# First MLP on one Trainium2 core: the down projection on 512-token tiles, the leftover 64 tokens of all batches as a ninth set, and second-MLP weight work in both stages

## The chip, the core and the metric

One NeuronCore of a Trainium2 chip runs the whole program in one launch. The metric is the device time of the launch in microseconds (us), the median of the runs shown. TensorE (PE; its weight loads are shown as PEld) multiplies, ScalarE (ACT) and VectorE (DVE) work on the elements, GpSimd (POOL) does next to nothing here, and SyncE (SP) issues most DMAs; some are issued from ScalarE's queue.

## The reference

Three layers in a row, over 8 batches of 576 tokens, 8 heads of 64:

```python
p_packed = sm_attn(p, k, v)                 # 32 packed queries a head against 576 keys
x = sm_attn(q, p_packed, p_packed)          # 576 queries against the 32 packed ones
g = x @ w_gate                              # 4608 tokens, 512 -> 1536
x = silu(g) * (x @ w_val) @ w_out           # first MLP, 1536 -> 512
h = x @ w_in                                # second MLP, 512 -> 2048
return (h * np.cos(h)) @ w_out2             # 2048 -> 512
```

All in fp32. The result has 4608 rows of 512.

## The kernel before

**Products.** TensorE multiplies in fp32r. A value that must keep its precision is held as two parts, hi (rounded by ScalarE, `split`, line 85) and lo (the difference, made by VectorE), and a product is three matmuls (`PASSES`): hi by hi, hi by lo, lo by hi.

**First MLP.** The loop at line 591 goes over the batches b = 0 to 7, and each batch has two stages. The up stage (`a_up`, line 402) makes, for 12 groups f of 128 hidden features, gate and value products (line 433) of the two halves c of the 576 tokens, 288 columns a matmul; ScalarE makes the silu, VectorE the product h, and the split of h makes `g[f]`, a tile [128, 2, 576] with the hi and the lo part. The down stage (`a_down`, line 478) makes the output in 8 groups n: 4 output blocks o of 128 features by 2 halves c. One group is 12 f by 3 passes, 36 matmuls of 288 columns into one PSUM bank (line 493); ScalarE copies the bank out to the tile `x2e` (line 498) and stores it to the DRAM tensor `x2d` from its own queue (line 499).

**What rides in the down stage.** The attention of batch b+1 is cut into steps that the dictionary `steps` hangs ahead of the groups n: 0 `a_s1`, 2 `a_t`, 3 `a_pp`, 4 `a_ppt`, 5 `a_s2`, 6 `a_wp`. `a_s2` (line 223) begins a long chain that alternates between VectorE and ScalarE (transposes, maximum, exponential, sum, division, transpose, split) and ends in the tiles `a2`; `a_wp` makes the weights `wp` of the next up stage, which multiply the attention's output straight away. In the last batch the steps load `x2d` for the second MLP and split it (`load_x2`, `sums_x2`, `split_x2`). At n = 0 SP is given the loads of v and q of batch b+1 (n = 2 for q in batch 0).

**What rides in the up stage.** `extra` (line 450) is called 24 times in each up stage. In batch 0 it decodes first-MLP weights. In batches 1 to 6 it works on the weights of the second MLP, 64 blocks: every second call stores finished pieces to DRAM (`w2_store`), loads the next raw block (`w2_load`), does up to two waiting splits or sums (`w2_work`) and decodes the present block (`w2_decode`: two ScalarE and two VectorE operations); the other calls do up to one split or sum. `prefetch` loads p and k of the next batch.

**Order.** The whole body stands in `tc.manual_schedule()`: each engine and each DMA queue works in the order of the program text, and an instruction whose input, buffer or queue entry is not ready holds up everything behind it on its engine. Buffers come from pools with a fixed number of slots: 18 of tag "c" (`ct`: g, a2, wp, v and others), 12 of tag "m" (`mt`: k, q, transposed tiles, raw blocks and finished pieces of the second-MLP weights), 11 small ones (`ht`), 8 PSUM banks.

**Second MLP** (from line 735 on): for 6 chunks of 768 tokens, up products of 384 columns (line 685) and down products of 512 columns (line 700).

Of the kernel before, what the change touches and what calls it, by code (L numbers as in the profile page):

```python
# [21 lines left out]
NF1, NF2, KD = DF1 // 128, DF2 // 128, DM // 128  # L22
NPAIR = H // 2
HS = S // 2
NC = -(-S // 128)
SPAD = 128 * NC
TH = 384
# [13 lines left out]
def attention_mlp_kernel(ctx: ExitStack, tc: tile.TileContext, qT, kT, vP, pP, wgv, w1o, w2, out):  # L41
# [11 lines left out]
    dr = ctx.enter_context(tc.tile_pool(name="dr", bufs=1, space=bass.MemoryType.DRAM))  # L53

    x2d = dr.tile([KD, 128, NT], F32, name="x2d")
    w2u = dr.tile([NPF, 7, 128, 512], F32, name="w2u")
    w2d = dr.tile([NF2, 128, 2, 512], F32, name="w2d")

# [6 lines left out]
    def ct(shape, dt, name):  # L65
        return sb.tile(shape, dt, tag="c", name=name, bufs=CBUFS)

    def mt(shape, dt, name):
        return sb.tile(shape, dt, tag="m", name=name, bufs=12)

    def ht(shape, dt, name):
        return sb.tile(shape, dt, tag="s", name=name, bufs=SBUFS)

    def bank(shape, name):
        return ps.tile(shape, F32, tag="b", name=name)
# [237 lines left out]
    def w2_load(i):  # L313
        if i < 4 * NF2:
            w2_raw[i] = raw_words(mt, w2[i // 2, :, 256 * (i % 2):256 * (i % 2) + 256], 256)
# [15 lines left out]
    def w2_decode(i):  # L331
        w_ = ht([128, 256], F32, "w2f")
        t_ = ht([128, 256], F32, "w2t")
        decode_a(w2_raw[i], t_, w_)
        decode_b(w2_raw.pop(i), t_, w_)
        u, half = divmod(i, 2)
        if u >= NF2:
            w2_put(w_, w2d[u - NF2, :, :, 256 * half:256 * half + 256])
            return
        p, a = divmod(u, 2)  # L340
        to = [w2u[p, n].rearrange("p (x c) -> p x c", x=2) for n in range(7)]
        w2_f[a, half] = w_
        if (a, half) == (0, 0):
            w2_put(w_, to[0])
        elif (a, half) == (0, 1):
            w2_put(w_, to[4])
        elif (a, half) == (1, 0):
            w2_sum("s3", (0, 0), ALU.subtract, (1, 0), to[2])
        else:
            w2_sum("s1", (1, 0), ALU.add, (1, 1), to[3])  # L350
            w2_put(w_, to[5])
            w2_sum("s2", "s1", ALU.subtract, (0, 0), to[1])
            w2_sum("s4", (0, 1), ALU.subtract, "s2", to[6])

    def w2_work(n):
        for _ in range(n):
            if w2_todo:
                w2_todo.pop(0)()

    def w2_store():  # L360
        while w2_done:
            p, dst = w2_done.pop(0)
            SP.dma_start(out=dst, in_=p.bitcast(F32))
# [34 lines left out]
    def flush_split():  # L398
        while pend_split:
            pend_split.pop(0)()  # L400

    def a_up(b):
        g = []
        for f in range(NF1):
            gt = ct([128, 2, S], F32R, "g")
            g.append(gt)
            if b > 0:
                if f in (2, 6):
                    a_wp(b, (f // 2 + 1, f // 2 + 2))
                w = [wp[b, f // 2, u][:, :, f % 2] for u in range(2)]  # L410
            else:
                w = wp.pop((0, f))
            banks = [(bank([128, HS], "pg"), bank([128, HS], "pv")) for _ in range(2)]
            if b == 0:
                for u in range(2):
                    for c in range(2):
                        for o, p_ in zip((0, 128), banks[c]):
                            PE.matmul(  # L418
                                out=p_, lhsT=w[:, u, o:o + 128], rhs=a2[u][:, HS * c:HS * c + HS],
                                start=(u == 0), stop=(u == 1),  # L420
                            )
                    if u == (f == 0) and f + 1 < NF1:
                        a_wp0(f + 1)
            for c in range(2):
                sl = slice(HS * c, HS * c + HS)
                pg, pv = banks[c]
                for o, p_ in ((0, pg), (128, pv)):
                    n = 0
                    for u in range(2):
                        if b == 0:  # L430
                            continue
                        for (x, y) in PASSES:
                            PE.matmul(  # L433
                                out=p_, lhsT=w[u][:, x, o:o + 128], rhs=a2[u][:, y, sl],
                                start=(n == 0), stop=(n == 5),
                            )
                            n += 1
                if b == 0 and f > 0:
                    u_step(2, 1)
                s_ = ht([128, HS], F32, "silu")  # L440
                ACT.activation(out=s_, in_=pg, func=AF.Silu)  # L441
                flush_split()
                h_ = ht([128, HS], F32, "h")
                DVE.tensor_tensor(out=h_, in0=s_, in1=pv, op=ALU.mult)  # L444
                pend_split.append(lambda h_=h_, gt=gt, sl=sl: split(h_, gt[:, 0, sl], gt[:, 1, sl]))
                extra(b, f, c)
            prefetch(b, f)
        return g

    def extra(b, f, c):  # L450
        if b == 0:
            u_step(0, 1)
            u_step(1, 1)
            if f == 0:
                u_step(2, 1)
        elif b < B - 1:
            s_ = 24 * (b - 1) + 2 * f + c
            if s_ % 2 == 0 and s_ // 2 < 4 * NF2:
                w2_store()
                w2_load(s_ // 2 + 1)  # L460
                w2_work(2)
                w2_decode(s_ // 2)
            else:
                w2_work(1)

    def prefetch(b, f):
        n = b + 1
        if n >= B:
            return
        if f == 4:  # L470
            load_p(n)
            for j in range(NPAIR):
                load_k(n, j)
        if f == 9 and b == 0:
            for j in range(NPAIR):
                load_v(n, j)

    def a_down(b, g, steps):
        for n in range(8):
            for s_ in steps.get(n, ()):  # L480
                s_()
            if 0 < b < B - 1 and n == 0:
                for j in range(NPAIR):
                    load_v(b + 1, j)
            if b + 1 < B and n == (2 if b == 0 else 0):
                for j in range(NPAIR):
                    load_q(b + 1, j)
            o, c = n // 2, n % 2
            sl = slice(HS * c, HS * c + HS)
            acc = bank([128, HS], "o1")  # L490
            for f in range(NF1):
                for i, (x, y) in enumerate(PASSES):
                    PE.matmul(  # L493
                        out=acc, lhsT=wo[o, f // 4][:, x, f % 4, :], rhs=g[f][:, y, sl],
                        start=(f == 0 and i == 0), stop=(f == NF1 - 1 and i == 2),
                    )
            ev = ht([128, HS], F32, "x2e")
            ACT.activation(out=ev, in_=acc, func=AF.Copy)  # L498
            ACT.dma_start(out=x2d[o, :, S * b + HS * c:S * b + HS * c + HS], in_=ev)

    late = {}

# [49 lines left out]
    with tc.manual_schedule():  # L552
# [37 lines left out]

        for b in range(B):
            g = a_up(b)
            flush_split()
            flush_wo()
            w2_store()
            if b == 0:
                w2_load(0)
            n = b + 1
            steps = {}
            if n < B:  # L600
                steps = {
                    0: (lambda: a_s1(n),),
                    2: (lambda: a_t(n),),
                    3: (lambda: a_pp(n),),
                    4: (lambda: a_ppt(n),),
                    5: (lambda: a_s2(n),),
                    6: (lambda: a_wp(n, (0, 1)),),
                }
            else:
                gates.close()  # L610
                late["x"] = ctx.enter_context(tc.tile_pool(name="xs", bufs=1, side="right", reuse_waits="tile"))
                x_now = [new_xs() for _ in range(7)]
                steps = {0: (lambda: load_x2(0),)}
                for i in range(4):
                    steps[i + 1] = (lambda i=i: sums_x2(i),)

                for i, ns in enumerate(((0,), (3,), (2,), (1, 4), (5, 6))):
                    steps[i + 1] = steps.get(i + 1, ()) + tuple(lambda n=n: split_x2(n, x_now) for n in ns)
            if b == 0:
                for i, k in enumerate((1, 1, 2, 2, 1)):  # L620
                    steps[i] = steps.get(i, ()) + (lambda: u_step(0, 1), lambda: u_step(1, 1), lambda: u_step(2, 1)) * k
                steps[5] = (flush_wo,) + steps[5]
            a_down(b, g, steps)
# [215 lines left out]
```

## Time and profile before

| | us |
|---|---|
| median of 3 runs | 1488.43 (1488.20 to 1488.91) |
| the profiled execution, its own time | 1488.04 |
| its span, first to last instruction of the program | 1486.3 |
| part of the span before the second MLP begins | 738.4 |

The profile is of one execution; its time is that of the launch, 1.7 us more than the span. A row of busy time counts an engine as busy while an instruction of it runs; matmuls overlap their neighbours, so the duration of one is longer than the time from its start to the next one's. The chain of work that ended last is followed back from the last instruction and tells, piece by piece, what the end of the program waited for. In timelines the number in brackets is the idle time of the engine ahead of the row, and who ended it. Batches are counted from 0.

### The profile page before, as it was taken

The page shows a single profiled execution, that of the slowest core. Times are in us where ns is not written, and L with a number is a line of the kernel's source. Part 1 is how long each engine was busy: PE and PEld are TensorE (multiplying, and loading weights), DVE is VectorE, ACT ScalarE, POOL GpSimd, SP SyncE. Part 2 cuts the span into 40 slices and gives each one's busy share as a digit, 9 for nine tenths or more (in the row PEclk, how much of TensorE's full clock was granted, in tenths as well). Part 3 has the DMA queues.
Part 4 walks back from the last instruction along what each step waited for, and adds up shares of the span by engine and source line. Part 5 has one row for each costly group of instructions (what it writes and reads, how often), then busy time and mean ns, then how long its engine had stood idle before and what let it go on. Part 6 is the DMA issues. An engine that isn't in the chain of part 4 may idle for free.

```text
span 1486.3 us, 27615 instructions
## 1 busy us (share of the span) xinstructions
PE 1478.3 (99%) x10476; PEld 1338.7 (90%) x10476; DVE 985.8 (66%) x2048; ACT 839.4 (56%) x1917; POOL 3.0 (0%) x22
## 2 busy tenths in 40 slices
PE   9999999999999999999999999999999999999999
PEld 6689998999899998989989999999999999999997
DVE  6988749485673837355286866776686686677654
ACT  6986737375572736434284645656555564565642
POOL 0000000000000000000000000000000000000000
PEclk9999999999999999999999999999999999999999
DMA  8742616355162542201295586576667558556641
GB/s 328 260 156 86 239 46 226 117 173 195 52 194 75 161 136 89 80 22 43 92 393 178 181 288 197 178 241 204 215 191 256 180 180 290 195 179 195 206 161 43
DMA packets 129411, 257.14 MB, mean 173 GB/s; under 512 B 13568, under 2 KB 37120, under 8 KB 129280
## 3 DMA queue, kind: packets, MB, share of 16 engines
q1 hardware_dynamic: 120064, 245.94, 50.4%
q10 hardware_dynamic: 9216, 9.44, 1.8%
q8 instruction: 83, 1.36, 0.4%
q14 instruction: 48, 0.39, 0.1%
HBM read 213.39 MB, written 41.94 MB: 172 GB/s over the span
## 4 chain that ended last, share of the span: by engine, by line
PE 95%; DVE 2%; ACT 2%; DMA 1%; issue 0%; SPq 0%; ACTq 0%; DVEq 0%
PE acc L700 26%; PE p L685 23%; PE o L493 20%; PE pg L433 9%; PE pv L433 9%; PE wp L386 3%; PE pg L418 1%; PE pv L418 1%; PE pp L203 1%; PE s L229 1%; PE s L151 1%; PE wp L371 0%; DMA qt<-in_qT 0%; PE tp L192 0%; DMA vt<-in_vP 0%
## 5 line engine op out<-in xcount | busy, mean ns | idle before, releaser
L700 PE MATMUL acc<-wd,g 128*128 128x512 f32 x1728 | 413.8, 389 | 0.0
L685 PE MATMUL p<-xs,up 128*128 128x384 f32 x2016 | 372.9, 337 | 1.3 <-ACT p L760 1.3
L700 PEld LDWEIGHTS acc<-wd,g 128*128 128x128 f32 x1728 | 322.4, 188 | 57.1
L685 PEld LDWEIGHTS p<-xs,up 128*128 128x128 f32 x2016 | 353.7, 188 | 12.7 <-ACT p L760 1.6
L493 PEld LDWEIGHTS o<-g,wo 128*128 128x128 f32 x2304 | 306.7, 188 | 13.8 <-DVE d L250 5.0
L493 PE MATMUL o<-g,wo 128*128 128x288 f32 x2304 | 316.6, 296 | 0.3 <-DVE wo L87 0.2
L663 ACT ACTIVATE t<-c,quarter 128x384 f32<-128x384 f32 x144 | 88.4, 614 | 196.7 <-DVE c L773 191.0
L433 PE MATMUL pg<-a,wp 128*128 128x288 f32 x1008 | 162.4, 296 | 0.0
L433 PE MATMUL pv<-a,wp 128*128 128x288 f32 x1008 | 160.6, 294 | 0.0
L433 PEld LDWEIGHTS pg<-a,wp 128*128 128x128 f32 x1008 | 142.4, 188 | 11.7 <-ACT wp L86 8.4
L433 PEld LDWEIGHTS pv<-a,wp 128*128 128x128 f32 x1008 | 143.0, 188 | 0.0
L87 DVE TENSOR_TENSOR g<-h,g 128x288 fp32r<-128x288 f32 x192 | 87.5, 456 | 39.4 <-ACT g L86 39.2
L673 DVE TENSOR_TENSOR g<-t,g 128x384 fp32r<-128x384 f32 x192 | 106.0, 552 | 8.0 <-ACT g L660 7.8
L665 DVE TENSOR_TENSOR t<-t,k 128x384 f32<-128x384 f32 x192 | 106.1, 552 | 3.5 <-ACT k L669 1.8
L768 DVE TENSOR_TENSOR u<-v,p 128x384 f32<-128x384 f32 x48 | 26.6, 554 | 118.2 <-PE p L685 117.9
L441 ACT ACTIVATE silu<-pg 128x288 f32<-128x288 f32 x192 | 78.3, 408 | 42.0 <-PE pg L433 37.5
L666 ACT ACTIVATE t<-t 128x384 f32<-128x384 f32 x192 | 98.2, 512 | 2.6 <-DVE t L665 2.5
L498 ACT ACTIVATE x2e<-o 128x288 f32<-128x288 f32 x64 | 26.5, 413 | 128.3 <-PE o L493 127.9
L660 ACT ACTIVATE g<-t 128x384 fp32r<-128x384 f32 x192 | 98.5, 513 | 0.4 <-DVE t L671 0.4
L86 ACT ACTIVATE g<-h 128x288 fp32r<-128x288 f32 x192 | 85.0, 443 | 24.2 <-DVE h L444 23.8
L669 ACT ACTIVATE k<-t 128x384 int32<-128x384 f32 x192 | 98.2, 511 | 0.0
L444 DVE TENSOR_TENSOR h<-silu,pv 128x288 f32<-128x288 f32 x192 | 86.0, 448 | 16.1 <-PE pv L433 5.9
(95 smaller groups left out, 1346.9 us busy)
## 6 DMA issues: line engine op xcount, KB each, us to landing
up<-w2u SPq DMA_DIRECT2D x336, 256.0 KB, 3.2
wd<-w2d SPq DMA_DIRECT2D x96, 512.0 KB, 6.2
raw<-in_w SPq DMA_DIRECT2D x64, 256.0 KB, 3.2
w2u<-w2p SPq DMA_DIRECT2D x56, 256.0 KB, 2.2
raw<-in_wgv SPq DMA_DIRECT2D x24, 512.0 KB, 7.5
vt<-in_vP SPq DMA_DIRECT2D x32, 320.0 KB, 4.3
kt<-in_kT SPq DMA_DIRECT2D x32, 288.0 KB, 5.0
qt<-in_qT SPq DMA_DIRECT2D x32, 288.0 KB, 6.0
```

Of the source, the lines that this page charges most:

```text
L87: eng.tensor_tensor(out=lo, in0=src, in1=hi.bitcast(F32), op=ALU.subtract)
L433: PE.matmul(out=p_, lhsT=w[u][:, x, o:o + 128], rhs=a2[u][:, y, sl], start=(n == 0), stop=(n == 5),)
L444: DVE.tensor_tensor(out=h_, in0=s_, in1=pv, op=ALU.mult)
L493: PE.matmul(out=acc, lhsT=wo[o, f // 4][:, x, f % 4, :], rhs=g[f][:, y, sl], start=(f == 0 and i == 0), stop=(f == NF1 - 1 and i == 2),)
L660: ACT.activation(out=three["g"][:, 0, :], in_=three["t"], func=AF.Copy)
L663: ACT.activation(out=now["t"], in_=now["h"], func=AF.Identity, scale=1.0 / TWO_PI, bias=quarter)
L665: DVE.tensor_tensor(out=one_["t"], in0=one_["t"], in1=one_["k"], op=ALU.subtract)
L666: ACT.activation(out=one_["t"], in_=one_["t"], func=AF.Sin, scale=SIN_SCALE)
L669: ACT.activation(out=now["k"], in_=now["t"], func=AF.Copy)
L673: DVE.tensor_tensor(out=three["g"][:, 1, :], in0=three["t"], in1=three["g"][:, 0, :].bitcast(F32), op=ALU.subtract)
L685: PE.matmul(out=out, lhsT=w[:, u, 128 * k:128 * k + 128], rhs=x[:, v, k, :], start=(first and k == 0 and i == 0), stop=(last and k == 1 an ...
L700: PE.matmul(out=acc, lhsT=gs[p, a, t][:, x, o:o + 128], rhs=wd[j, f][:, y, :], start=(f == 0 and n == 0), stop=(f == 3 and n == 2),)
```

## The change

The down stage of a batch takes only the first 512 of its 576 tokens, as one tile: 4 groups a batch, one for each output block o, each of 36 matmuls of 512 columns. The bank is copied out in two halves of 256. The other 64 tokens of each `g[f]`, hi and lo, are stored by SP to a DRAM tensor `rest`, 24 DMAs of 32 KB a batch in pieces of 256 bytes. For batches 0 to 6 they are issued in the down stage, after the loads of v and q, at the middle of the first group (for batch 7 during its up stage, each f one turn late). From the up stage of batch 7 on SP also loads the set back as tiles of 8 x 64 = 512 tokens (`load_rest`, 24 DMAs of 256 KB; those of the last three f behind the end of that stage), and `a_rest` runs the down projection on this ninth set ahead of the down stage of batch 7. The attention steps keep their numbers: step n now comes at f = 0 or f = 6 of the group o = n // 2. The second-MLP weight work keeps its 24 calls a batch, 16 of them in the up stage (two of three turns), 8 in the down stage (f = 3 and f = 9 of each group).

```diff
@@ -22,6 +22,8 @@
 NF1, NF2, KD = DF1 // 128, DF2 // 128, DM // 128
 NPAIR = H // 2
 HS = S // 2
+WIN = 512
+REST = S - WIN
 NC = -(-S // 128)
 SPAD = 128 * NC
 TH = 384
@@ -53,6 +55,7 @@
     dr = ctx.enter_context(tc.tile_pool(name="dr", bufs=1, space=bass.MemoryType.DRAM))
 
     x2d = dr.tile([KD, 128, NT], F32, name="x2d")
+    rest = dr.tile([NF1, 2, 128, B, REST], F32, name="rest")
     w2u = dr.tile([NPF, 7, 128, 512], F32, name="w2u")
     w2d = dr.tile([NF2, 128, 2, 512], F32, name="w2d")
 
@@ -398,6 +401,8 @@
     def flush_split():
         while pend_split:
             pend_split.pop(0)()
+
+    gr = []
 
     def a_up(b):
         g = []
@@ -445,7 +450,24 @@
                 pend_split.append(lambda h_=h_, gt=gt, sl=sl: split(h_, gt[:, 0, sl], gt[:, 1, sl]))
                 extra(b, f, c)
             prefetch(b, f)
+            if b == B - 1 and f > 0:
+                store_rest(b, f - 1, g[f - 1])
+                if f > 2:
+                    gr.append(load_rest(f - 3))
         return g
+
+    w2_n = [0]
+
+    def w2_step():
+        s_ = w2_n[0]
+        w2_n[0] += 1
+        if s_ % 2 == 0 and s_ // 2 < 4 * NF2:
+            w2_store()
+            w2_load(s_ // 2 + 1)
+            w2_work(2)
+            w2_decode(s_ // 2)
+        else:
+            w2_work(1)
 
     def extra(b, f, c):
         if b == 0:
@@ -453,15 +475,8 @@
             u_step(1, 1)
             if f == 0:
                 u_step(2, 1)
-        elif b < B - 1:
-            s_ = 24 * (b - 1) + 2 * f + c
-            if s_ % 2 == 0 and s_ // 2 < 4 * NF2:
-                w2_store()
-                w2_load(s_ // 2 + 1)
-                w2_work(2)
-                w2_decode(s_ // 2)
-            else:
-                w2_work(1)
+        elif b < B - 1 and (2 * f + c) % 3 < 2:
+            w2_step()
 
     def prefetch(b, f):
         n = b + 1
@@ -475,28 +490,68 @@
             for j in range(NPAIR):
                 load_v(n, j)
 
+    def store_rest(b, f, gt):
+        for i in range(2):
+            SP.dma_start(out=rest[f, i, :, b, :], in_=gt[:, i, WIN:S].bitcast(F32))
+
+    def load_rest(f):
+        if f < NF1 // 2:
+            r = [mt([128, B, REST], F32R, "gr") for _ in range(2)]
+        else:
+            both = ct([128, 2, B, REST], F32R, "gr")
+            r = [both[:, i] for i in range(2)]
+        for i in range(2):
+            SP.dma_start(out=r[i].bitcast(F32), in_=rest[f, i])
+        return r
+
+    def down_group(o, moving, steps, to, between=None):
+        acc = bank([128, WIN], "o1")
+        for f in range(NF1):
+            if f % (NF1 // 2) == 0:
+                for s_ in steps.get(2 * o + f // (NF1 // 2), ()):
+                    s_()
+            if between and f % 6 == 3:
+                between()
+            for i, (x, y) in enumerate(PASSES):
+                PE.matmul(
+                    out=acc, lhsT=wo[o, f // 4][:, x, f % 4, :], rhs=moving(f, y),
+                    start=(f == 0 and i == 0), stop=(f == NF1 - 1 and i == 2),
+                )
+        for h in range(2):
+            ev = ht([128, WIN // 2], F32, "x2e")
+            ACT.activation(out=ev, in_=acc[:, WIN // 2 * h:WIN // 2 * h + WIN // 2], func=AF.Copy)
+            to(o, h, ev)
+
     def a_down(b, g, steps):
-        for n in range(8):
-            for s_ in steps.get(n, ()):
-                s_()
+        def to(o, h, ev):
+            c0 = S * b + WIN // 2 * h
+            ACT.dma_start(out=x2d[o, :, c0:c0 + WIN // 2], in_=ev)
+
+        def loads(n):
             if 0 < b < B - 1 and n == 0:
                 for j in range(NPAIR):
                     load_v(b + 1, j)
             if b + 1 < B and n == (2 if b == 0 else 0):
                 for j in range(NPAIR):
                     load_q(b + 1, j)
-            o, c = n // 2, n % 2
-            sl = slice(HS * c, HS * c + HS)
-            acc = bank([128, HS], "o1")
-            for f in range(NF1):
-                for i, (x, y) in enumerate(PASSES):
-                    PE.matmul(
-                        out=acc, lhsT=wo[o, f // 4][:, x, f % 4, :], rhs=g[f][:, y, sl],
-                        start=(f == 0 and i == 0), stop=(f == NF1 - 1 and i == 2),
-                    )
-            ev = ht([128, HS], F32, "x2e")
-            ACT.activation(out=ev, in_=acc, func=AF.Copy)
-            ACT.dma_start(out=x2d[o, :, S * b + HS * c:S * b + HS * c + HS], in_=ev)
+            if b < B - 1 and n == 1:
+                for f in range(NF1):
+                    store_rest(b, f, g[f])
+
+        steps = {n: tuple(steps.get(n, ())) + (lambda n=n: loads(n),) for n in range(8)}
+        for o in range(KD):
+            down_group(o, lambda f, y: g[f][:, y, 0:WIN], steps, to, w2_step if 0 < b < B - 1 else None)
+
+    def a_rest(gr):
+        def to(o, h, ev):
+            half = B // 2
+            ACT.dma_start(
+                out=x2d[o].rearrange("p (b n) -> p b n", b=B)[:, half * h:half * h + half, WIN:S],
+                in_=ev.rearrange("p (b n) -> p b n", b=half),
+            )
+
+        for o in range(KD):
+            down_group(o, lambda f, y: gr[f][y].rearrange("p b n -> p (b n)"), {}, to)
 
     late = {}
 
@@ -595,6 +650,12 @@
             w2_store()
             if b == 0:
                 w2_load(0)
+            if b == B - 1:
+                for f in range(len(gr), NF1):
+                    if f == NF1 - 1:
+                        store_rest(b, f, g[f])
+                    gr.append(load_rest(f))
+                a_rest(gr)
             n = b + 1
             steps = {}
             if n < B:
```

## Rows read from the trace of the kernel before

**Rows 1.** The page: span, share of TensorE, and the chain that ended last.

```profile
span 1486.3 us, 27615 instructions
...
PE 1478.3 (99%) x10476; PEld 1338.7 (90%) x10476; DVE 985.8 (66%) x2048; ACT 839.4 (56%) x1917; POOL 3.0 (0%) x22
...
PE 95%; DVE 2%; ACT 2%; DMA 1%; issue 0%; SPq 0%; ACTq 0%; DVEq 0%
```

**Rows 2.** Chain, down of batch 6 to up of 7: start us, us, what.

```profile
613.59 9.74 PE o L493 x72
...
640.37 1.13 PE s L229 x32
641.50 4.99 PE o L493 x36
646.49 1.88 PE wp L386 x32
648.37 9.74 PE o L493 x72
658.10 0.79 PE pg L433 x6
```

**Rows 3.** The same chain, whole span: last down stage, and one 512-wide group.

```profile
700.40 38.16 PE o L493 x288
...
764.61 2.72 PE acc L700 x12
```

**Rows 4.** Busy time by stage, the up stages of batches 2, 3 and 5.

```profile
216.87:260.83 43.96, 43.96 (x385) 39.54 (x384) 40.34 (x105) 34.78 (x98) 0.31 (x2) 1.00 0.64 212
...
305.42:349.44 44.02, 44.02 (x385) 39.54 (x384) 40.41 (x105) 34.96 (x97) 0.31 (x2) 1.00 0.61 205
...
482.22:525.58 43.36, 43.36 (x385) 39.45 (x383) 35.16 (x86) 34.18 (x89) 0.31 (x2) 1.00 0.50 155
```

**Rows 5.** Timeline of ScalarE and VectorE, end of the down stage of batch 6.

```profile
652.82 0.69 ACT L86 ACTIVATE a<-af 128x576 fp32r<-128x576 f32 x1 [3.66 <-DVE af L252]
653.41 0.39 ACT L498 ACTIVATE x2e<-o 128x288 f32<-128x288 f32 x1
...
654.20 2.07 ACT L86 ACTIVATE wp<-wp 128x512 fp32r<-128x512 f32 x4 [0.40 <-ACT x2e L498]
654.83 2.48 DVE L87 TENSOR_TENSOR wp<-wp 128x512 fp32r<-128x512 f32 x4 [0.54 <-ACT wp L86]
```

**Rows 6.** Groups by line: the hi half of a second-MLP weight split.

```profile
L86 ACT ACTIVATE w2p<-w2f 128x256 fp32r<-128x256 f32 x56 | 23.3, 415 | 7.7 <-DVE w2f L108 7.5
```

**Rows 7.** Timeline of the SP queue, the loads at the start of that stage.

```profile
612.13 1.75 SPq L132 DMA_DIRECT2D vt<-in_vP  x4
613.93 2.02 SPq L128 DMA_DIRECT2D qt<-in_qT  x4
```

**Rows 8.** DMA issues: line engine op xcount, KB each, us to landing.

```profile
raw<-in_w SPq DMA_DIRECT2D x64, 256.0 KB, 3.2
w2u<-w2p SPq DMA_DIRECT2D x56, 256.0 KB, 2.2
...
qt<-in_qT SPq DMA_DIRECT2D x32, 288.0 KB, 6.0
...
xb<-x2d SPq DMA_DIRECT2D x24, 384.0 KB, 5.5
```

**Rows 9.** Timeline, last down stage: last g split, x2 splits, weight loads.

```profile
701.82 0.46 DVE L87 TENSOR_TENSOR g<-h,g 128x288 fp32r<-128x288 f32 x1 [0.51 <-ACT g L86]
...
726.83 0.95 DVE L87 TENSOR_TENSOR xs<-xb,xs 128x768 fp32r<-128x768 f32 x1
729.05 19.12 SPq L544 DMA_DIRECT2D up<-w2u  x21
```

**Rows 10.** SP's own waits: weight loads held by landings of ScalarE's stores.

```profile
SPq L544 <- DMA x2d<-x2e: 14.2, 4, 5.7
```

**Rows 11.** The page's DMA queues: packets, MB, share of 16 engines.

```profile
q10 hardware_dynamic: 9216, 9.44, 1.8%
```

## The prediction, written before the changed kernel was run

> **What bounds the kernel now.** I read the page first: TensorE is busy 99% of the span and holds 95% of the chain that ended last [rows 1]. So what counts is how long TensorE works, and whether a change makes it wait. Next the chain in order of time, through one down stage of the first MLP and into the next up stage [rows 2]: every piece but the start of the small steps is a run of matmuls, with no gap between a group of the down projection and the attention step that rides in it. VectorE and ScalarE are hidden there, as long as each step's result is ready when TensorE comes to it. The last down stage, which has no attention steps, gives the clean price of a matmul of 288 columns: 288 of them in 38.16 us, 132.5 ns each; the second MLP gives that of 512 columns: 12 in 2.72 us, 226.7 ns [rows 3].
>
> **1. Fewer, wider matmuls: -11.5 us.** Before: 8 batches x 8 groups x 36 = 2304 matmuls of 288 columns. After: 8 x 4 x 36 for the batches and 4 x 36 for the ninth set, 1296 of 512. The columns are the same, 663,552; what falls away is the part of a matmul's price that doesn't grow with its columns, 1008 times. A batch goes from 38.16 us to 144 x 0.2267 = 32.64 us. 8 x 38.16 = 305.3 becomes 9 x 32.64 = 293.8 [rows 3]: 11.5 us less, all on the path. The granted clock is 1.00, the level of 2.4 GHz, in the up stages shown [rows 4], and I take both prices at that level.
>
> **2. Second-MLP weight work moved: -1.3 us.** The up stages of batches 2 and 3 take 43.96 and 44.02 us, that of batch 5 43.36 us with the lighter half of that work [rows 4]; VectorE is busy 40 of 44 us there and holds TensorE a little. With 16 calls instead of 24 these 0.60 + 0.66 us should go (0 to 1.3). The calls that leave cost TensorE nothing by themselves; what they delay in the down stage is in 3 and 4.
>
> **3. The down stage gets shorter, its chain of steps doesn't: +2.7 us.** From `a_s2` (640.37) to the first up matmul (658.10) TensorE now takes 17.7 us, of it one group of 4.99 and two of 9.74 together [rows 2]. With half groups of 18 x 0.2267 = 4.08 us this is 1.13 + 4.08 + 0.25 (what 4.99 has over 4.74) + 1.88 + 8.16 + 0.26, 15.8 us: TensorE comes 2.0 us earlier to the up stage. What it needs there ends with the split of `wp`: VectorE's four parts start at 654.83 and take 2.48 us, so the second of them, needed by the sixth or so matmul (658.77), is there at 656.07, 2.7 us ahead [rows 5]. ScalarE's side also gets longer: two copies of `x2e` instead of one lie ahead of the `wp` splits, 0.79 us each with their store (653.41 to 654.20) [rows 5], and in batches 1 to 5 one weight split, 0.41 us [rows 6]. 2.7 - 2.0 - 0.79 - 0.41 = -0.5: a wait of 0.5 us in five batches, and of 0.1 us in batches 0 and 6: 2.7 us together. Ends: 0, and 1.5 us each in all seven (if ScalarE's further calls push the next stage's silu as well), 10.5 us.
>
> **4. The 24 stores on SP's queue: +2.5 us.** They come behind eight loads, three stores of finished pieces and a raw load, and ahead of the next raw load, which the decode at f = 3 of o = 2 waits for; behind that decode stand, on ScalarE and VectorE, the transposes of `a_s2`. When is it wanted? `a_s2` now comes 26.78 us behind the first down matmul, 23.7 of it five groups [rows 2]; five halves of 4.08 make it 23.5 us, and f = 3 lies 2.04 before: 21.4 us. When does it land? The eight loads start 1.4 us ahead of the first down matmul and take SP 3.8 us, 0.44 to 0.50 each [rows 2, 7]. At 0.50: 2.4 us, four more DMAs to 4.4, 24 stores to 16.4, three stores and the load to 18.4, landing 3.2 us later [rows 8], 21.6 us. That is within 0.2 us of when it is wanted, so the cover is thin. I take 0.5 us in each of batches 1 to 5, 2.5 us; ends: 0 (0.44 each: 19.7 us) and the first rival's 18.5 us. The stores themselves need only `g`, long done. In batch 0 the last two raw blocks of `w_out` stand behind them; they have the two spare steps up to `a_s2`, and I count 0 (to 2 us).
>
> **5. The ninth set waits for its last piece: +3.0 us.** The last `g` split ends at 702.28, 2.0 us into the stage that follows [rows 9]. Its two stores: 0.9 us to issue, 2.2 to land (nearest row: a store of 256 KB); its two loads: 0.9 and 3.2 [rows 8]: 9.2 us behind the up stage's end. `a_rest` comes to its last f after 33 x 0.2267 = 7.5 us: 1.8 us of wait, once. Four of the last tiles find no free slot until the up stage has ended (12 g, 2 a2 and 4 wp or loaded tiles fill the 18), so six loads of 256 KB stand ahead in the same queue. With 6.0 us, the slowest landing of [rows 8], for both, it would be 8.4 us. I take 3.0, nearer the first, since those six are issued some 3 us before.
>
> **6. Counted at nothing.** The x2 load for the second MLP moves behind the ninth set: 0.8 us to copy out, 2.2 to store, 5.5 to load [rows 8], 8.5 us of a 32.6 us stage; its splits ended 10.6 us before the stage did (727.78 of 738.4) [rows 9] and have no other work beside them. Without that cover it would be the 8.5 us. The first second-MLP weights are loaded from 729.05, when the o = 2 groups end, 9.3 us ahead of use [rows 9]; now 8.2 us, against a landing of 3.2 [rows 8]; without cover, the 1.1 us. 8 copies more on ScalarE lie beside TensorE.
>
> **Sum.** -11.5 - 1.3 + 2.7 + 2.5 + 3.0 = -4.6 us against the profiled execution's 1488.04 (span 1486.3 and 1.7 around it): 1483.4. The median shown, 1488.43, is 0.4 above that execution, so 1483.8. 0.2%, about what a measurement of this kernel tells from no change, is 3.0 us.
>
> **The rivals.** *SP holds the decode (slower, 0.22).* The place is the raw load of 4. If the stores can't start before the eight loads have landed (the last is issued at 615.95 and takes 6.0 us [rows 7, 8], 8.4 us into the stage), 24 x 0.50, four more DMAs and 3.2 us bring the load to 25.6 us, 4.2 late, 3.7 beyond what 4 counts: 5 x 3.7 = 18.5 us, 1502. It decides from about 1 us of lateness in each batch on: five times that eats the gain. For it: SP's queue does wait for earlier landings [rows 10]. Against it: a store has a ninth of a load's bytes.
>
> *ScalarE's own stores queue behind them (slower, 0.05).* A store of `x2e` at the end of o = 0 that has to wait for landings, as SP's loads do for ScalarE's stores, up to 5.7 us [rows 10], would hold `a_t`'s copies: 5 us x 7, some 1519.
>
> *The pieces of 256 bytes are slow (slower, 0.04).* ScalarE's queue moved 9216 packets of about 1 KB in 1.8% of 16 engines' span, 46 ns each [rows 11]; at that price a store's 8 pieces an engine take 0.37 us, less than SP's 0.50. No row shows a piece of 256 bytes. At twice that, 92 ns, the 24 take 17.7 us in place of 12, the raw load lands 5.7 us later, 5.9 late, and five batches cost 27 us more than 4 counts: 1511. The Trainium skill, "DMA: Bandwidth & Descriptors", section "Specifications", speaks for this: below 512 bytes a transfer is read, modified and written. By the packet row alone the stores stay hidden.
>
> *Waits cancel the gain (0.13).* 3, 4 and 5 together some 4 to 7 us more: 1486 to 1491.
>
> *The whole gain (0.1).* 3 to 5 cost nothing: 1475.6. That the columns don't get cheaper is as good as excluded by [rows 3].
>
> **Numbers.** Forecast 0.46, its own range 1479 to 1487. Range for 8 in 10: 1477 to 1500; what is left out is half of the whole gain, the upper half of the first rival, and the two dear ones. Faster by over 0.2%: 0.40 + 0.1 = 0.50. Within: 0.06 of the forecast, 0.10 of the cancelled, 0.04 of the first rival, 0.20. Slower: 0.30.
>
> **What would show it.** 1: 1296 matmuls, 0.227 us apart. 2: up stages of batches 2 and 3 at 43.4 us. 3: a gap of half a us ahead of the first up matmul, ended by a `wp` split. 4: no wait of ScalarE for a raw block over 1 us in the down stages. 5: one gap of 2 to 4 us in the ninth set. Gaps of several us in each down stage would prove the forecast wrong, and so would a second MLP that starts later by more than this sum.

## The result and the profile after

The changed kernel takes 1497.85 us (median of 4 runs, 1496.2 to 1501.04), the kernel of before beside it 1488.32: ratio 1.0066, 95% interval 1.0049 to 1.0084. It was forecast 0.3% faster and is 0.7% slower. The profiled run takes 1497.66 us against 1488.04, so +9.6 where the sum said -4.6.

The page of the changed kernel, the lines that answer to [rows 1]:

```profile
span 1495.8 us, 25963 instructions
...
PE 1477.0 (99%) x9468; PEld 1276.2 (85%) x9468; DVE 988.0 (66%) x2048; ACT 840.9 (56%) x1925; POOL 3.0 (0%) x22
...
PE 81%; DVE 6%; DMA 4%; SPq 4%; ACT 4%; issue 1%; ACTq 0%; DVEq 0%
```

TensorE is still "99% busy"; that line doesn't show the loss. The chain does: TensorE held 95% of it, now 81%, and VectorE, DMAs, SP's queue and ScalarE have taken its place. The second MLP starts at 747.6 us (738.4 before) and takes 0.4 us longer than it did, so nearly all of the loss lies ahead of it. Busy time by stage (columns as in [rows 4]: window, its length, TensorE's busy time, then its weight loads, VectorE, ScalarE, GpSimd, each with its count; granted clock, DMA share, GB/s); a down stage runs from its first matmul of the down projection to the first of the next up stage, so a wait ahead of an up stage counts in the down stage before it. These are the down stages of batches 0 and 2 to 5, the ninth set, and the down stage of batch 7:

```profile
83.73:127.62 43.89, 40.73 (x309) 30.16 (x301) 33.14 (x65) 27.29 (x57) 0.00 (x0) 1.00 0.40 123
255.06:294.51 39.45, 39.31 (x309) 30.10 (x301) 22.10 (x54) 17.44 (x43) 0.00 (x0) 1.00 0.53 173
339.09:379.64 40.55, 39.31 (x308) 30.09 (x300) 22.59 (x55) 17.89 (x45) 0.00 (x0) 1.00 0.51 163
423.95:465.15 41.20, 39.31 (x308) 30.09 (x300) 18.44 (x43) 16.03 (x39) 0.00 (x0) 1.00 0.43 134
510.79:551.23 40.44, 39.31 (x309) 30.09 (x301) 18.57 (x43) 16.03 (x39) 0.00 (x0) 1.00 0.44 136
677.74:714.97 37.23, 34.98 (x147) 27.82 (x145) 1.28 (x3) 2.95 (x8) 0.00 (x0) 0.95 0.33 97
714.97:747.61 32.64, 32.64 (x146) 27.04 (x145) 10.10 (x11) 8.66 (x15) 0.00 (x0) 1.00 0.35 110
```

The last line is the forecast's price, 32.64 us for 144 matmuls. The down stages of batches 1 and 6 take 39.14, which is what a stage with its attention steps costs undisturbed; before it was 44.4. Everything above that is waiting. The chain of waits through the down stage of batch 5 into the next up stage, in order of time (start us, us, what):

```profile
515.08 5.39 DMA rest<-g
...
530.91 0.52 SPq L366
...
531.48 3.24 DMA raw<-in_w
534.74 0.46 ACT w2t L101
...
536.45 1.57 DVE d L239 x4
...
550.58 0.61 ACT wp L89
551.21 0.70 DVE wp L90
551.95 1.00 PE pg L438 x4
```

In place of the unbroken matmuls of [rows 2] the chain runs through a store of `rest`, the rest of that block on SP's queue (left out here), a raw block, the decode (L101), `a_s2`'s VectorE steps (L239 on), the split of `wp`, and only then into the up stage. SP's timeline of that stage (start us, us, what):

```profile
514.32 0.41 SPq L94 DMA_DIRECT2D raw<-in_w  x1
515.08 15.74 SPq L495 DMA_DIRECT2D rest<-g  x24
...
531.48 0.60 SPq L94 DMA_DIRECT2D raw<-in_w  x1
```

The block of 24 stores holds the queue for 15.7 us, and the raw block behind it is issued 20.7 us after the stage's first matmul. ScalarE's waits that a DMA ended (us in total, times, longest):

```profile
ACT w2t L101 <- DMA raw<-in_w: 8.5, 5, 3.2
ACT ET L197 <- DMA rest<-g: 2.8, 3, 1.9
ACT dec L101 <- DMA raw<-in_w1o: 2.5, 1, 2.5
```

The first line is those raw blocks, five times, in batches 1 to 5; the last is batch 0's last raw blocks of `w_out`, behind the stores in the same queue.

### The profile page after: what moved, and what is told of

It is laid out like the page before. It is cut to its first block, busy times and chain, and to the rows that moved or that the text cites. A ratio compares the mean times of both kernels' runs of the same rounds, so it can differ in the third digit from the quotient of the medians.

```text
span 1495.8 us, 25963 instructions
## 1 busy us (share of the span) xinstructions
PE 1477.0 (99%) x9468; PEld 1276.2 (85%) x9468; DVE 988.0 (66%) x2048; ACT 840.9 (56%) x1925; POOL 3.0 (0%) x22
## 4 chain that ended last, share of the span: by engine, by line
PE 81%; DVE 6%; DMA 4%; SPq 4%; ACT 4%; issue 1%; ACTq 0%; DVEq 0%
PE acc L761 26%; PE p L746 22%; PE pg L438 9%; PE pv L438 9%; PE o L516 8%; SPq L495 2%; PE wp L389 2%; DMA rest<-g 2%; PE pg L423 1%; PE pv L423 1%; DMA raw<-in_w 1%; DVE af L255 1%; DVE d L253 1%; DVE d L239 1%; DVE d L243 1%
## 5 line engine op out<-in xcount | busy, mean ns | idle before, releaser
L516 PE MATMUL o<-g,wo 128*128 128x512 f32 x1152 | 273.6, 394 | 0.0
L516 PEld LDWEIGHTS o<-g,wo 128*128 128x128 f32 x1152 | 213.1, 188 | 56.1 <-issue 4.6
L438 PE MATMUL pg<-a,wp 128*128 128x288 f32 x1008 | 167.2, 300 | 6.1 <-ACT wp L89 4.7
L775 DVE TENSOR_TENSOR oacc<-oacc,acc 128x512 f32<-128x512 f32 x108 | 73.7, 683 | 32.2 <-PE acc L761 32.1
```

The costliest lines, as they stand in the source:

```text
L438: PE.matmul(out=p_, lhsT=w[u][:, x, o:o + 128], rhs=a2[u][:, y, sl], start=(n == 0), stop=(n == 5),)
L516: PE.matmul(out=acc, lhsT=wo[o, f // 4][:, x, f % 4, :], rhs=moving(f, y), start=(f == 0 and i == 0), stop=(f == NF1 - 1 and i == 2),)
```

## The experiments

Three theories. **Q**: the block of stores holds SP's queue, and a raw block behind it comes too late. **S**: the shorter stage is too short for its own chain of steps, whatever the queue does. **Ninth set**: its wait for the last piece, with the clock. All times are medians; "before" is the kernel of before, run beside them (medians of 1487.78 to 1488.12).

| run | us | ratio to before, 95% interval |
|---|---|---|
| before, weight work spread (before_spread) | 1486.33 | 0.9990 [0.9981, 0.9999] |
| after, weight work in the up stage (w2_in_up) | 1492.99 | 1.0038 [1.0026, 1.0051] |
| after, stores one by one (stores_spread) | 1489.98 | 1.0013 [1.0004, 1.0021] |
| after, 12 stores (stores_paired) | 1489.45 | 1.0009 [1.0000, 1.0017] |
| after, ninth set later (ninth_after_one) | 1491.32 | 1.0025 [1.0016, 1.0034] |
| after, ninth set kept busy (ninth_busy) | 1494.57 | 1.0045 [1.0033, 1.0058] |
| stores one by one + ninth set later (both_moves) | 1484.55 | 0.9977 [0.9968, 0.9986] |
| + `a_s2` earlier (three_moves) | 1483.18 | 0.9967 [0.9955, 0.9979] |
| + weight work in two groups (four_moves) | 1482.11 | 0.9961 [0.9948, 0.9975] |
| + 12 late stores (five_moves) | 1483.25 | 0.9965 [0.9952, 0.9979] |
| after, weight work in two groups (w2_first_block) | 1528.95 | 1.0277 [1.0263, 1.0291] |

**One part alone, on the kernel of before.** `extra` keeps 16 calls of 24, and each of the eight 288-column groups gets one:

```diff
-        elif b < B - 1:
+        elif b < B - 1 and (2 * f + c) % 3 < 2:
...
             for f in range(NF1):
+                if 0 < b < B - 1 and f == 6:
+                    w2_step()
```

> The kernel of before with one part of the change alone: the second-MLP weight work at 16 calls in the up stage and 8 in the down stage, one in the middle of each of the eight 288-column groups. Prediction's point 2: 1.3 us less, 1487. Theory Q: the same or a little less, since SP's queue is free in that kernel's down stage: 1486.5 to 1488.5. Theory S (decodes, splits and raw waits in the down stage delay the chain of steps by themselves): 1 to 2 us a batch over six batches, 1494 to 1500.

1486.33, 1.5 us faster. Its up stage of batch 3, by busy time; that of batch 2 takes as long:

```profile
304.49:348.01 43.52, 43.52 (x386) 39.61 (x384) 37.29 (x95) 32.40 (x86) 0.31 (x2) 1.00 0.51 176
```

43.52 in both. [rows 4] begin 0.16 us later in the stage; cut as here, the two stages took 44.12 and 44.18 us, so they give 1.26 us. In the down stage of this kernel, still 44.4 us long, decodes and raw loads do no harm by themselves.

**The opposite: the changed kernel without that part.**

```diff
-        elif b < B - 1 and (2 * f + c) % 3 < 2:
+        elif b < B - 1:
             w2_step()
...
-            down_group(o, lambda f, y: g[f][:, y, 0:WIN], steps, to, w2_step if 0 < b < B - 1 else None)
+            down_group(o, lambda f, y: g[f][:, y, 0:WIN], steps, to)
```

> The changed kernel with all 24 calls of the second-MLP weight work back in the up stage, none in the down stage; the 512 columns, the stores and the ninth set stay. Theory Q (the block of 24 stores holds SP's queue, so that the raw block behind it reaches ScalarE late): no decode stands in the down stages 1 to 6 any more, so the 1.5 to 2.3 us that stages 3, 4 and 5 lose go, 5 to 6 us in all, and the up stages cost at most 1 us more: 1492 to 1494. Theory S (the stage of 40.8 us is too short for its own chain of steps, whatever the queue does): with less work in the stage the chain ends earlier as well, but the half-us to one-us waits at the start of the up stages stay: 1494 to 1497. Theory M (moving the work is worth 1.3 us as predicted and the loss is elsewhere): 1499.

1492.99, as theory Q had it. The block of stores is still there, but no decode waits behind it, and the down stages 1 to 6 take 39.12 to 39.20 us; that of batch 4, 41.20 in the changed kernel, by busy time:

```profile
424.62:463.76 39.14, 39.14 (x309) 30.26 (x301) 17.69 (x41) 14.48 (x35) 0.00 (x0) 1.00 0.43 132
```

Against the expectation, the up stages of batches 2 and 3 took 45.4 and 45.8 us: with 24 calls there, VectorE finishes that work after the matmuls and holds the scores (`s`) of the next step. (The profiled execution took 1495.12 us, 2.1 above the median; its ninth set took 39.2 us, with the granted clock at 0.50 over 4 us and 0.70 over the next 3.5.) So a change that gains 1.5 us on the kernel of before costs some 5 us beside the block: they collide.

**The stores one by one**, one every second weight tile (the last argument picks the hi or the lo half):

```diff
-            if b < B - 1 and n == 1:
-                for f in range(NF1):
-                    store_rest(b, f, g[f])
...
+            if each and f % 2:
+                each(6 * o + f // 2)
...
+        each = (lambda k: store_rest(b, k // 2, g[k // 2], (k % 2,))) if b < B - 1 else None
```

> The changed kernel with the 24 stores of batches 0 to 6 issued one by one, one every second weight tile of the down stage, in place of a block at its second eighth. Theory Q: the raw blocks (of w_out in batch 0, of the second MLP's weights in the others) no longer stand behind 24 stores, and no ScalarE wait for raw over 1 us is left in the down stages; batch 0 gives back 3 to 4 us and batches 2 to 5 together 5 to 6: 1488 to 1490. Theory S: the steps are late without the block too, under 3 us come back: 1495 to 1498.

1489.98. The decodes' waits for a second-MLP raw block are gone (a copy of `ET` still waits for one in two batches, 1.1 us at most): the group of decodes on ScalarE (busy, mean ns of one | idle before) reads

```profile
L101 ACT ACTIVATE w2t<-raw 128x256 f32<-128x256 f32 x64 | 27.6, 432 | 0.0
```

and the down stages of batches 2 to 5 take 39.15 to 39.46, batch 0 42.13 in place of 43.89: 1.8 us back, where 3 to 4 were expected. The ninth set got longer here, 39.18 us; the granted clock was at 0.50 over 4 us of it and at 0.73 over the next 4.

**The block with half as many stores**, the same bytes in the same 256-byte pieces:

```diff
-        for i in range(2):
-            SP.dma_start(out=rest[f, i, :, b, :], in_=gt[:, i, WIN:S].bitcast(F32))
+        SP.dma_start(
+            out=rest[f, :, :, b, :].rearrange("i p n -> p i n"), in_=gt[:, :, WIN:S].bitcast(F32)
+        )
```

> The changed kernel with one store for both halves of a g tile: 12 stores of 64 KB in a batch's block in place of 24 of 32 KB, the block still at the second eighth; bytes and pieces stay the same. Theory Q as a matter of issues (each store holds SP's queue for 0.43 to 0.47 us): the block lasts 5 to 6 us less, the raw block lands before the step chain needs it, and nearly all that the spread stores gave back comes here too: 1489 to 1492. Theory Q as a matter of bytes (the queue is held because the pieces of 256 bytes have to land): a store holds twice as long, nothing comes back: 1496 to 1498.

1489.45: what the spread stores gave comes here too. SP's timeline in the down stage of batch 5:

```profile
506.72 0.67 SPq L94 DMA_DIRECT2D raw<-in_w  x1
507.43 10.09 SPq L494 DMA_DIRECT2D rest<-g  x12
...
518.19 0.60 SPq L94 DMA_DIRECT2D raw<-in_w  x1
```

The block lasts 10.1 us, not 15.7, and the raw block is issued 14.8 us into the stage (503.42), not 20.7. Bytes and pieces are the same, so they are not what the block costs: 12 DMAs fewer at some 0.47 us make the 5.7 us. The waits at the head of the block, for landings of the loads ahead, are still there.

**The ninth set.** In the changed kernel's chain, its wait for the last piece:

```profile
680.82 4.58 DMA rest<-g
...
685.46 2.62 DMA gr<-rest
...
688.12 32.00 PE o L516 x133
```

and by busy time the clock around that wait:

```profile
684.00:688.00 4.00, 1.87 (x7) 0.79 (x5) 0.00 (x0) 0.00 (x0) 0.00 (x0) 0.97 0.45 153
688.00:691.50 3.50, 3.38 (x8) 2.53 (x9) 0.00 (x0) 0.77 (x2) 0.00 (x0) 0.54 0.07 23
```

Two edits. One puts the set behind the first group of the last down stage, with x2's loads and splits two eighths later; the other fills the wait with nine matmuls of zeros (`g0` is true for the ninth set alone):

```diff
         for o in range(KD):
+            if b == B - 1 and o == 1:
+                a_rest(gr)
...
-                a_rest(gr)
...
-                steps = {0: (lambda: load_x2(0),)}
+                steps = {2: (lambda: load_x2(0),)}
```

> The changed kernel with the ninth set between the first and the second 512-column group of the last batch's down stage, in place of ahead of it; the loads of x2 and the splits behind them come two eighths later. The last piece then has 8 us more to arrive. If the ninth set's 4.6 us over 144 matmuls are its wait for the last piece and the half-level clock that follows the wait, they all go and the time is 1493 to 1494. If only the wait goes and the clock falls anyway, 1495 to 1496. If the later splits make the second MLP's first matmuls late, that takes back up to 3 us.

```diff
+            if o == 0 and not between and g0 and f == NF1 - 1:
+                keep_busy(9)
```

> The changed kernel with nine matmuls of zeros into a spare bank in the ninth set, ahead of the matmuls on the last piece, where TensorE waits 2.3 us. They add no wait if they end before the piece lands. If the fall of TensorE's granted clock to its half level (0.54 over 3.5 us) comes from that wait, it stays away, and the ninth set takes 1.6 us less than 37.2: 1496. If the clock falls there for another reason: 1497.5 to 1498.5.

The ninth set in the first (1491.32 us) and in the second (1494.57 us), busy time by stage:

```profile
684.47:717.11 32.64, 32.64 (x146) 27.04 (x144) 0.00 (x0) 3.08 (x8) 0.00 (x0) 1.00 0.25 68
```

```profile
674.71:710.77 36.06, 35.65 (x165) 29.04 (x163) 1.28 (x3) 2.95 (x8) 0.00 (x0) 1.00 0.34 99
```

Moved, it costs its matmuls and nothing else: 4.6 us less, and x2's later splits delay nobody. Filled, the clock stays at 1.00 and the set takes 1.2 us less, short of the 1.6 expected. In all five profiled executions that keep the gap (2.3 to 2.5 us from start to start; the changed kernel, w2_in_up, stores_spread, stores_paired, w2_first_block) the clock fell in it or right behind it. Both medians lie 2 us below what that explains. That part isn't in the ninth set: their block stages were less late than the changed kernel's (down stages 3 to 5 add up to 122.2 us in the one profile quoted above, to 121.2 and 119.4 here), and kernels with late stages vary more from run to run: the first of these two by 6.5 us over 11 runs, the next kernel by 0.9 over 10.

**Together**, the diffs of the spread stores and of the later ninth set:

> Spread stores and the ninth set behind the last batch's first group together. The two causes lie in different stages, so their gains should add, and the ninth set of the run with spread stores, 39.2 us for 144 matmuls, should come down to 32.6: 1489.98 less 6.5 is 1483.4; 1482 to 1485. If the stores merely move their trouble (TensorE waits for x2's loads or the second MLP's first weights instead), 1486 to 1488.

1484.55, 0.2% faster than before: the two gains add. Then `a_s2` a quarter group earlier (a step at f = 3 of o = 2):

```diff
-                    5: (lambda: a_s2(n),),
+                    5 if b == 0 else 4.5: (lambda: a_s2(n),),
```

> As the run before it, and the step a_s2 of batches 2 to 7 issued a quarter group (three weight tiles, 2 us) earlier in the down stage of batches 1 to 6. Theory S for what is left: each of six up stages starts with 0.4 to 1.2 us of waits for wp's last split, because the chain from a_s2 to that split takes 14.8 us and the three last eighths of the shorter stage 14; issued 2 us earlier it ends in time, and 0.7 us come back six times: 1478 to 1480.5. If the wait at the stage's start is of another kind (ScalarE's own order of x2e copies and splits), nothing or up to 1 us comes back: 1482.5 to 1484.

1483.18: only 1.4 of some 4 us. The chain into the up stage of batch 6 shows why:

```profile
537.68 0.76 DVE a L90
538.44 0.42 DVE w2f L108
...
539.34 0.03 ACT w2p L89
...
539.67 0.38 ACT x2e L527
...
541.25 0.61 ACT wp L89
...
541.88 0.70 DVE wp L90
...
542.62 1.00 PE pg L438 x4
```

The step came earlier, and a decode and a weight split (`w2f`, `w2p`) slipped between `a2` and the copies of `x2e`, ahead of the `wp` splits. Next, those calls only in the first two groups:

```diff
-            if between and f % 6 == 3:
+            if between and o < 2 and f % 3 == 1:
```

> As the run with three moves, and the eight calls of second-MLP weight work of a down stage all in its first two groups (at weight tiles 1, 4, 7 and 10) in place of two in each of the four groups. With three moves a decode and a split of w2p still stood between the last split of a2 and the copies of x2e on ScalarE, ahead of wp's splits. Theory S, as a matter of ScalarE's order: without them wp's last split ends 1.5 to 2 us earlier, and the up stages of batches 2 to 6 start without a wait: 0.4 to 0.8 us each, 1479.5 to 1481.5. If the wait has another source: 1483.

1482.11, the fastest here, but above the 1479.5 to 1481.5 expected. The up stages of batches 2 to 6 all start on time, as theory S had it, and take 2.4 us less together; the down stages give 1.2 us of that back. Two of the up stages by busy time:

```profile
209.58:253.10 43.52, 43.52 (x385) 39.60 (x384) 36.48 (x93) 32.68 (x87) 0.31 (x2) 1.00 0.48 164
...
458.89:502.41 43.52, 43.52 (x385) 39.60 (x383) 32.87 (x80) 31.64 (x82) 0.31 (x2) 1.00 0.38 122
```

The same one-line edit on the changed kernel, whose block of stores stands where it stood:

> The changed kernel, its block of 24 stores where it was, with the eight calls of second-MLP weight work of a down stage in its first two groups as in the run with four moves. Theory Q: now decodes whose raw block is issued behind the block of stores stand on ScalarE ahead of the copies of ET, x2e and ppT, so every step behind them is late by some 5 us or more in each of six batches; the rival of the prediction as it was priced, slower than the changed kernel: 1505 to 1530. Theory S alone (the chain at the stage's end, no queue): less work at the end, faster than the changed kernel: 1493 to 1496.

1528.95, in the range of theory Q and 31 us over the changed kernel, but mostly by another wait than theory Q named. ScalarE's waits:

```profile
ACT x2e L522 <- DMA rest<-g: 30.1, 5, 6.6
ACT w2t L101 <- DMA raw<-in_w: 14.6, 8, 3.1
```

Five times ScalarE's queue stood up to 6.6 us until a store of `rest` had landed, ahead of its own store of `x2e`, and the copies of `ET` behind it made `a_pp` late: that is the prediction's second rival, priced at 5 us a batch. Late raw blocks are the smaller part.

Last, the run with four moves had raw waits left (down stages 1, 4 and 5 at 39.65, 40.46 and 39.56), so the 12 paired stores went into groups 3 and 4:

```diff
-            if each and f % 2:
-                each(6 * o + f // 2)
+            if each and f % 2 and o > 1:
+                each(6 * (o - 2) + f // 2)
...
+        each = (lambda k: store_rest(b, k, g[k])) if b < B - 1 else None
```

> As the run with four moves, with one store for both halves of a g tile, and the 12 stores of a batch one by one in the third and fourth group of the down stage, where no raw block is wanted any more. In the run with four moves the down stages 1, 4 and 5 still took 39.65, 40.46 and 39.56 us in place of 39.14. Theory Q: these are again raw blocks and copies of ET behind stores on SP's queue; with the queue free in the first half they go: 2.2 us less, 1479.5 to 1481. If those waits come from the loads of vt and qt themselves, or from the landings, nothing comes back: 1481.5 to 1483.

1483.25: a miss, no better than four moves. Batch 1 is back at 39.14, but batches 4 and 5 take 40.87 and 39.85. The chain of batch 4's down stage, with no store in that half:

```profile
422.10 0.99 SPq L131
...
423.14 6.31 DMA raw<-in_w
...
429.47 0.44 ACT w2t L101
```

The raw block now stands behind the eight loads of `vt` and `qt` alone, and lands 6.3 us after its issue: the rival that the expectation names.

## Why the prediction was wrong

Inside its range, on the wrong side. It counted the removed work rightly and the added waits 14.2 us too low. By its own steps:

**1, right.** The matmuls, groups by line (busy, mean ns | idle before): 1152 + 144 are the 1296 forecast, and the last down stage ran at 32.64 us. The whole 11.5 us were there.

```profile
L516 PE MATMUL o<-g,wo 128*128 128x512 f32 x1152 | 273.6, 394 | 0.0
...
L516 PE MATMUL o<-gr,wo 128*128 128x512 f32 x144 | 35.1, 404 | 2.2 <-DMA gr<-rest 2.1
```

**2, right as a term, lost in the sum.** Alone it gives 1.5 us (1.3 forecast), and with the waits gone the up stages take 43.52 again. In the changed kernel those of batches 2 and 3 took 44.00 and 44.59, because point 3 ate it.

**3, right in kind, too small.** The wait is there, ended by a `wp` split; timeline of TensorE at the start of batch 7's up stage (in brackets: idle before):

```profile
634.67 0.52 PE L438 MATMUL pg<-a,wp 128*128 128x288 f32 x2
635.38 1.00 PE L438 MATMUL pg<-a,wp 128*128 128x288 f32 x4 [0.19 <-DVE wp L90]
```

42.30 became 43.06 even in that stage, whose down stage has no weight work: 0.76 us where 0.1 was forecast, and the others took 0.5 to 1.1 more than 43.52, without the clock's share in batch 5. The slip is one of small sizes where the sum had left 0.1 between supply and need. The second copy of `x2e` put the `wp` splits 1.05 us later, not 0.79 (1.84 us from the first copy to the first split, 632.17 to 634.01, against the 0.79 of [rows 5]), and TensorE waited for VectorE's first part already. Points 2 and 3 together were +1.4 us; the seven up stages grew by 5.2, of it 1.3 in batch 5 from the clock that fell behind a wait.

**4, the step that failed.** "24 stores to 16.4" took 0.50 us a store. The stores were issued at that rate only once the loads ahead had landed; until then each waited for a landing, and in batch 5 one took 2.4 us. SP's waits ahead of these stores (us in total, times, longest):

```profile
SPq L495 <- DMA qt<-in_qT: 11.2, 19, 1.1
SPq L495 <- DMA vt<-in_vP: 6.5, 13, 1.3
```

The trace's semaphore records show why a store that needs only `g` waits for a load: all 1072 DMAs of the program, SP's and ScalarE's alike, take turns on eight completion semaphores, 134 on each, and none was issued before the last one with its semaphore had landed, so never more than eight were in flight. The first stores of the block thus wait for the loads, and a store of `x2e` on ScalarE's queue can wait for a store of `rest`. The block ended 20.0 us into the stage and not 16.4, the raw block landed at 23.9 and not 21.6, and ScalarE, which came for it at 21.4 as forecast, waited 2.6. That is the first rival's mechanism (stores that can't start before the loads have landed), at under a third of its price: there the raw load landed at 25.6 in every batch; here ScalarE's raw waits sum to 8.5 us in five. Down stages 1 to 6 cost 6.5 us more than before less 5.5 each; 2.5 was forecast. (1.4 of the 6.5 is the 0.24 us by which even a stage of 39.14 lies above that; 5.1 is waiting.)

**Batch 0** was counted at 0 (to 2 us) and cost 4.2: 1.8 of it is the raw block of `w_out` behind the stores (it comes back with the spread stores), some 2.4 stays in every version. With the stores spread the chain through that stage waits for no DMA; it is ScalarE's and VectorE's work, decodes and splits of `w_out` between the attention steps, and TensorE waits 0.5 us for `E`, 0.3 for `ET` and 1.0 for `wp`: theory S again, by its trace; no run took that work out.

**5, right in kind, one price left out.** One gap, 2.3 us beyond the spacing, was inside the 2 to 4 forecast (3.0 in the sum; the 1.8 worked out there from 9.2 and 7.5 is 1.7). Not counted: a second price, the clock at its half level behind the gap. 4.6 us instead of 3.0.

**6, right.** The second MLP started without a wait, even with x2's splits two eighths later.

The three misses (6.5 and 4.2 for 2.5 in the down stages, 5.2 for 1.4 in the up stages, 4.6 for 3.0) make 13.6 of the 14.2 us; the rest is spread over the start and the second MLP.

**The rivals.** *ScalarE's own stores*: in the changed kernel a landing of `rest` held ScalarE ahead of the `ET` copies three times, 1.9 us at most (the waits shown first); one line's edit away it was 30 us. *Pieces of 256 bytes* did no harm; DMA issues (KB each, us to landing):

```profile
rest<-g SPq DMA_DIRECT2D x192, 32.0 KB, 1.6
gr<-rest SPq DMA_DIRECT2D x24, 256.0 KB, 2.8
```

A store of 32 KB lands in 1.6 us, less than the 2.2 of a 256 KB store [rows 8]. The Trainium skill, "DMA: Bandwidth & Descriptors", section "Specifications", has transfers under 512 bytes read, modified and written; if that costs anything here, it doesn't show in these landings, nor in the packet records of the trace: the 24,576 pieces of 256 bytes took 18 ns each, pieces of 1024 bytes 46 ns. The rival's price was 92.

What is left in the fastest version against the ideal: batch 0's 2.4 us, 0.8 at the start of batch 1's up stage, 0.2 in every down stage and 2.3 of raw blocks behind the loads. Whether another order of those loads frees the last was not tried.

## What to carry to other kernels

A DMA that only has to be issued "some time" still occupies its queue: count the issues, look for what is wanted behind them and by which in-order engine, find out how many may be in flight at once (eight here, over both queues), and let such DMAs trickle in one by one rather than in a block. When a stage gets shorter, walk its longest chain of small steps engine by engine, in the order of each engine's queue; its slack was the matmul time that you removed. Two changes that are each harmless, or good, can collide in one queue, so test each alone and both together.

## What the runs showed of the hardware

The granted clock fell to its half level (1.2 GHz) right behind the gap in the ninth set, 2.5 us from one matmul's start to the next (0.54 over 3.5 us, above), and behind one of 2.3 us ahead of batch 5's up stage, which took 45.64 us where its neighbours take 44.30:

```profile
465.90:469.40 3.50, 3.50 (x15) 3.50 (x16) 2.90 (x6) 2.09 (x6) 0.00 (x0) 0.51 0.38 100
```

A gap of 2.2 us in batch 0 left its stage at 1.00. The length of the gap alone doesn't tell, though: ahead of the same up stage the clock fell behind gaps of 1.9 us (ninth_after_one, 45.62 us) and 1.6 us (ninth_busy, 45.83 us), while one of 1.8 us ahead of batch 4's (ninth_after_one) left that stage at 44.30. Nine matmuls of zeros in the ninth set's wait kept the clock at 1.00. The Trainium skill, "TensorE: Matmul & The Clock Gate", section "Part 1: The HAM clock gate", says that the gate goes by how busy TensorE has lately been, and names these two levels; the rows agree in that every fall ahead of the second MLP came at a gap, and batch 0's gap shows that not every wait has this price. Where it has, as in batch 5's up stage (1.3 us behind 2.3), it adds more than half of the wait again.
